# Loading and transposing the first x rows of a fused MLP backward kernel in tiles of 128, 128 and 256 rows, on two queues

## Chip, cores, metric

The kernel runs on one core of a Trainium2 chip. The metric is the device time of one execution in microseconds (us). All executions quoted here are fast: none lies over 1.5% above the fastest of its kernel. A trace starts at the first instruction of the core, and its span is about 1.8 us shorter than the execution's time.

The engines go by short names in the profiles: PE is TensorE (PEld its loading of weights), DVE is VectorE, ACT is ScalarE, POOL is GpSimd, and SP is SyncE. A load is issued by the queue of an engine, here SyncE or ScalarE; it has landed when the profile shows its last part complete. The matmuls of this kernel write to banks of the memory called PSUM, from which DVE or ACT copies the results to SBUF.

## The reference

The reference computes a two-layer MLP with SiLU and all its gradients, in bfloat16, with 2048 rows, width 640 and hidden width 1536:

```
h   = silu(x @ w1)          # x: 2048 x 640, w1: 640 x 1536
out = h @ w2                # w2: 1536 x 640
returns out, and the gradients of x, w1, w2 for a given grad_out
```

## The kernel before

The matmuls of `x @ w1` take x with its columns on the 128 partitions, so x has to be turned first. The kernel works in four chunks of 512 rows. For later chunks a transposing DMA turns x (three of them in the trace of this kernel, 7.4 us from issue to landing in the median) and TensorE does not wait for it. For the first chunk that would be too late, as an estimate from the same trace, whose first 128x512 matmul starts at 5.01 us: its rows are loaded plainly and turned on TensorE with an identity. Before they land, matmuls on a tile of ones run as a warm-up for the clock of TensorE (with them it was full from 3.6 us in the trace below). The head of the kernel is this:

```python
NWARM = 22
warm = cpool.tile([P, P], dt_in, name="warm")
early = [nc.vector.memset(warm[:], 1.0)]
for i in range(NWARM):
    early.append(nc.tensor.matmul(wp[:, 0:P], lhsT=warm[:], rhs=warm[:], start=True, stop=True))
...
def load_x_half(half):
    lo = half * 2 * P
    return nc.sync.dma_start(
        out=x_two[:, half, :, :], in_=x2[lo:lo + 2 * P, :].rearrange("(p q) d -> p q d", q=2)
    )
...
early += [load_x_half(0), load_x_half(1), load_w1_rows(0, 1), load_w1_rows(1, KM)]
load_w1_rows(KM, DT)                         # KM = 2, DT = 5 row blocks of w1
start_before_entry_wait(nc, {i.ins.name for i in early})
for fc in range(1, NFC):
    load_w1(fc * FC, (fc + 1) * FC)          # 640 KB each
...
def pe_x_half(xT, half):
    lo = half * 2 * P
    for dt_ in range(DT):
        tp = ps_h.tile([P, 2, P], dt_in, name="tp", tag="hp")
        for q in range(2):
            nc.tensor.transpose(tp[:, q, :], x_two[:, half, q, dt_ * P:(dt_ + 1) * P], ident[:])
        copy = nc.scalar.copy if dt_ % 2 else nc.vector.tensor_copy
        copy(out=xT[:, dt_, lo:lo + 2 * P].rearrange("p (s q) -> p q s", q=2), in_=tp[:])
```

The first 128x512 matmuls (`hp<-xT,w_nat`) follow: row block 0 of w1 for four output tiles, then row block 1 for the four, then the rest. `start_before_entry_wait` moves the early instructions ahead of the barrier at the start of the program.

## Time and profile before

| | us |
|---|---|
| time, median of 3 (range) | 321.21 (321.15 to 321.69) |
| span of the trace | 318.9 |
| x halves land (trace) | 3.03 and 4.00 |
| w1 row blocks 0, 1, 2-4 land | 4.34, 5.20, 6.22 |
| first 128x512 matmul starts | 5.01 |
| last matmul starts | 315.79 |

The trace is of one more execution, of 320.68 us, which is not among the three.

The page of the kernel before, its line of TensorE's busy time (busy us, share of the span, instructions) and its chain of work that ended last, by engine and by line:

```profile
PE 315.2 (99%) x1498; PEld 145.4 (46%) x1498; DVE 102.2 (32%) x182; ACT 77.7 (24%) x142; POOL 0.7 (0%) x6
...
PE 98%; DMA 1%; DVE 1%; issue 0%; DVEq 0%; SPq 0%
```

TensorE (PE) is the limit. From 5.01 us on it has no gap, so a change to the head can gain only what it takes off the start of the first 128x512 matmul. Here is that head: the timeline of PE in the kernel before from 0 to 11 us (start, length, what, count, and in brackets how long PE was idle before the group and for whom):

```profile
0.50 2.53 PE L125 MATMUL wp<-warm 128*128 128x128 bf16 x22 [0.50 <-DVE warm L121]
3.08 1.70 PE L177 MATMUL tp<-ident,x_two 128*128 128x128 bf16 x20
5.01 6.20 PE L186 MATMUL hp<-xT,w_nat 128*128 128x512 bf16 x28 [0.23 <-DVE xT L179]
```

The 22 warm-up matmuls, the 20 transposes and then the stream of 128x512 matmuls stand nearly back to back. The longest idle time that the timeline gives between them is the 0.23 us before the first 128x512 matmul, which waits for the last needed copy of DVE. One more line is needed later, from the groups by line and form of the kernel before, window 5.5 to 8.9 us (after the bar: busy us, mean ns of one):

```profile
L186 PE MATMUL hp<-xT,w_nat 128*128 128x512 bf16 x18 | 4.0, 379 | 0.0
```

A 128x512 matmul has a recorded length of 379 ns and starts come 216 ns apart: this is called full clock here. For a 128x128 matmul the starts are 56 ns apart at full clock and 107 at half. In this trace they change from 107 to 56 at 3.6 us.

### The profile page before, as it was taken

What the parts mean: (1) busy time and instruction counts of PE and PEld (TensorE: products, weight loads), DVE (VectorE), ACT (ScalarE), POOL (GpSimd) and SP (SyncE); (2) the same over time, 40 slices, a digit from 0 to 9 for tenths busy, and PEclk for the clock granted to TensorE, in tenths of its full rate; (3) what the DMA queues carried; (4) which work ended last, traced back from release to release, by engine and by line L of the source; (5) the groups of instructions that cost most, each with busy time, mean ns of one, the idle gap of its engine ahead of it and who ended that gap; (6) DMA issues with size and microseconds to landing.
All of it is one profiled execution on the core that took longest, in us unless ns stands there. A gap on an engine that the chain in (4) does not pass through costs nothing.

```text
span 318.9 us, 3570 instructions
## 1 busy us (share of the span) xinstructions
PE 315.2 (99%) x1498; PEld 145.4 (46%) x1498; DVE 102.2 (32%) x182; ACT 77.7 (24%) x142; POOL 0.7 (0%) x6
## 2 busy tenths in 40 slices
PE   9999999999999999999999999999999999999996
PEld 6444444444444444444444444444444444444443
DVE  2871641477410187700157741000001100001001
ACT  4951000644201354311065410111000001001100
POOL 0000000000000000000000000000000000000000
DMA  8999999998999866382643089719999998995011
GB/s 274 319 173 221 250 243 277 334 289 264 290 288 305 199 200 166 109 286 82 166 128 119 2 279 264 200 45 285 272 207 270 262 249 288 239 293 194 34 48 34
DMA packets 147311, 67.33 MB, mean 211 GB/s; under 512 B 112608, under 2 KB 147040, under 8 KB 147296
## 3 DMA queue, kind: packets, MB, share of 16 engines
q1 hardware_dynamic: 147296, 67.12, 81.5%
q8 instruction: 11, 0.18, 0.2%
q14 instruction: 4, 0.03, 0.0%
HBM read 9.83 MB, written 28.97 MB: 122 GB/s over the span
## 4 chain that ended last, share of the span: by engine, by line
PE 98%; DMA 1%; DVE 1%; issue 0%; DVEq 0%; SPq 0%
PE hp L249 32%; PE hp L186 16%; PE hp L337 16%; PE hp L233 16%; PE hp L385 15%; PE hp L367 1%; DMA x_two<-in_x_dram 1%; DVE xT L179 0%; PE tp L177 0%; DVE g L378 0%; DVEq L378 0%; SPq L413 0%
## 5 line engine op out<-in xcount | busy, mean ns | idle before, releaser
L186 PE MATMUL hp<-xT,w_nat 128*128 128x512 bf16 x240 | 56.9, 379 | 0.2 <-DVE xT L179 0.2
L233 PE MATMUL hp<-goT,w2T 128*128 128x512 bf16 x240 | 56.9, 379 | 0.0
L249 PE MATMUL hp<-aT,w_nat 128*128 128x512 bf16 x240 | 52.5, 379 | 0.0
L249 PE MATMUL hp<-ghT,w1T 128*128 128x512 bf16 x240 | 52.5, 379 | 0.0
L337 PE MATMUL hp<-a_blk,go_nat 128*128 128x512 bf16 x240 | 52.0, 379 | 0.0
L385 PE MATMUL hp<-gh_blk,x_nat 128*128 128x512 bf16 x224 | 48.5, 379 | 0.0
L257 ACT ACTIVATE oT<-hp 128x512 bf16<-128x512 f32 x24 | 14.3, 597 | 109.8 <-PE hp L249 109.8
L195 ACT ACTIVATE aT<-hp 128x512 bf16<-128x512 f32 x48 | 29.9, 625 | 32.8 <-PE hp L186 32.8
L186 PEld LDWEIGHTS <-w_nat 128*128 128x128 bf16 x240 | 23.5, 98 | 28.4 <-issue 0.4
L233 PEld LDWEIGHTS <-w2T 128*128 128x128 bf16 x240 | 23.5, 98 | 28.3
L337 PEld LDWEIGHTS <-go_nat 128*128 128x128 bf16 x240 | 23.5, 98 | 28.3
L249 PEld LDWEIGHTS <-w1T 128*128 128x128 bf16 x240 | 23.5, 98 | 28.3
L249 PEld LDWEIGHTS <-w_nat 128*128 128x128 bf16 x240 | 23.4, 98 | 28.3
L259 DVE CAST oT<-hp 128x512 bf16<-128x512 f32 x16 | 11.1, 692 | 77.0 <-PE hp L249 77.0
L240 DVE SCALAR_TENSOR_TENSOR ghT<-ghT,hp 128x512 bf16<-128x512 bf16 x48 | 32.5, 681 | 7.3 <-PE hp L233 7.3
L385 PEld LDWEIGHTS <-x_nat 128*128 128x128 bf16 x224 | 21.9, 98 | 26.4
L202 DVE SCALAR_TENSOR_TENSOR ghT<-aT,v 128x512 bf16<-128x512 bf16 x48 | 32.7, 686 | 0.5
L201 DVE TENSOR_SCALAR v<-t 128x512 bf16<-128x512 f32 x48 | 20.2, 425 | 30.1 <-ACT t L199 30.1
L199 ACT ACTIVATE t<-hp 128x512 f32<-128x512 f32 x48 | 29.8, 625 | 0.0
L396 DVE CAST g<-hp 128x512 bf16<-128x512 f32 x7 | 4.8, 691 | 47.1 <-PE hp L385 27.6
L347 DVE CAST g2T<-hp 128x512 bf16<-128x512 f32 x7 | 4.8, 692 | 46.1 <-PE hp L337 46.1
L345 ACT ACTIVATE g2T<-hp 128x512 bf16<-128x512 f32 x8 | 4.8, 597 | 47.0 <-PE hp L337 47.0
(20 smaller groups left out, 25.2 us busy)
## 6 DMA issues: line engine op xcount, KB each, us to landing
aT_scr<-aT SPq DMA_DIRECT2D x4, 1536.0 KB, 7.1
ghT_scr<-ghT SPq DMA_DIRECT2D x4, 1536.0 KB, 8.0
out_dram<-o_sb SPq DMA_DIRECT2D x8, 640.0 KB, 3.6
oT_scr<-oT SPq DMA_DIRECT2D x4, 640.0 KB, 3.6
go_nat<-in_grad_out_dram SPq DMA_DIRECT2D x4, 640.0 KB, 6.6
x_nat<-in_x_dram SPq DMA_DIRECT2D x4, 640.0 KB, 5.4
gxT_scr<-oT SPq DMA_DIRECT2D x4, 640.0 KB, 4.7
w_nat<-in_w_dram SPq DMA_DIRECT2D x1, 1920.0 KB, 13.7
```

The costliest lines, as they stand in the source:

```text
L186: nc.tensor.matmul(hp[:], lhsT=w1_nat[:, dt_, ft * P:(ft + 1) * P], rhs=xT[:, dt_, :], start=(dt_ == 0), stop=(dt_ == DT - 1),)
L195: nc.scalar.activation(aT[:, ft, :], hp[:], ACT.Silu)
L199: nc.scalar.activation(t[:], hp[:], ACT.Tanh, scale=0.5)
L201: nc.vector.tensor_scalar(out=v[:], in0=t[:], scalar1=-0.5, scalar2=0.5, op0=ALU.mult, op1=ALU.add)
L202: nc.vector.scalar_tensor_tensor(out=ghT[:, ft, :], in0=aT[:, ft, :], scalar=1.0, in1=v[:], op0=ALU.subtract, op1=ALU.mult)
L233: nc.tensor.matmul(gp[:], lhsT=w2T[:, dt_, ft * P:(ft + 1) * P], rhs=goT[:, dt_, :], start=(dt_ == 0), stop=(dt_ == DT - 1),)
L240: nc.vector.scalar_tensor_tensor(out=ghT[:, ft, :], in0=ghT[:, ft, :], scalar=1.0, in1=gp[:], op0=ALU.add, op1=ALU.mult)
L249: nc.tensor.matmul(op_[:], lhsT=w_all[:, ft, dt_ * P:(dt_ + 1) * P], rhs=rhs_all[:, ft, :], start=(ft == 0), stop=(ft == FT - 1),)
L257: nc.scalar.activation(oT[:, dt_, :], op_[:], ACT.Copy)
L259: nc.vector.tensor_copy(out=oT[:, dt_, :], in_=op_[:])
L337: nc.tensor.matmul(gp[:], lhsT=go_nat[:, st, dt_ * P:(dt_ + 1) * P], rhs=a_blk[:, st, :], start=(st == 0), stop=(st == ST - 1),)
L385: nc.tensor.matmul(gp[:], lhsT=x_nat[:, st, dt_ * P:(dt_ + 1) * P], rhs=gh_blk[:, st, :], start=(st == 0), stop=(st == ST - 1),)
```

## The change

Its intent is to start turning x sooner: a first tile of 128 rows needs half the bytes of the first half of before, a second queue takes part of the loads, and fewer, joint copies empty the PSUM banks. The rows land directly in `x_nat`, which needs them at the end anyway, so one later 640 KB load goes away. The load of w1 rows 2-4 also joins the early ones. The diff, cut to its core:

```diff
-    NWARM = 22
+    NWARM = 17
+    NFILL = 2
...
-        early += [load_x_half(0), load_x_half(1), load_w1_rows(0, 1), load_w1_rows(1, KM)]
-        load_w1_rows(KM, DT)
+        early += [
+            load_x_tiles(nc.sync, 0, 1),
+            load_x_tiles(nc.scalar, 1, 2),
+            load_x_tiles(nc.sync, 2, STC),
+            load_w1_rows(nc.scalar, 0, KM),
+            load_w1_rows(nc.sync, KM, DT),
+        ]
...
+        def turn(out, st, dt_):
+            nc.tensor.matmul(
+                out, lhsT=x_nat[:, st, dt_ * P:(dt_ + 1) * P], rhs=ident[:], start=True, stop=True
+            )
+
+        def pe_x_tile(xT, st):
+            for copy, lo, hi in ((nc.vector.tensor_copy, 0, KM), (nc.scalar.copy, KM, DT)):
+                tp = ps_h.tile([P, hi - lo, P], FP32, name="tp", tag="hp")
+                for dt_ in range(lo, hi):
+                    turn(tp[:, dt_ - lo, :], st, dt_)
+                copy(out=xT[:, lo:hi, st * P:(st + 1) * P], in_=tp[:])
... (pe_x_pair: two tiles as pe_x_half before, with float32 banks and plain matmuls)
-        pe_x_half(xT_next, 0)
-        pe_x_half(xT_next, 1)
+        pe_x_tile(xT_next, 0)
+        pe_x_tile(xT_next, 1)
+        for i in range(NFILL):
+            nc.tensor.matmul(wp[:, 0:P], lhsT=warm[:], rhs=warm[:], start=True, stop=True)
+        pe_x_pair(xT_next, 2)
...
-                for j in range(0, ST, STC):
+                for j in range(STC, ST, STC):      # the later load of x_nat
```

The two fillers are written between tile 1 and tiles 2-3, but they depend on nothing, and the scheduler puts them ahead of tile 0. They are two more warm-up matmuls.

More of the change, by code (lines that the diff above doesn't have):

```diff
@@ L145, with load_x_tiles, load_w1_rows @@
         xT_next = xpool.tile([P, DT, SC], dt_in, name="xT")
-        x_two = cpool.tile([P, 2, 2, D], dt_in, name="x_two")
         def load_w1(lo, hi):
             nc.sync.dma_start(out=w1_nat[:, :, lo:hi], in_=w1_v[:, :, lo:hi])
-        def load_x_half(half):
-            lo = half * 2 * P
-            return nc.sync.dma_start(
-                out=x_two[:, half, :, :], in_=x2[lo:lo + 2 * P, :].rearrange("(p q) d -> p q d", q=2)
-            )
-        def load_w1_rows(lo, hi):
-            return nc.sync.dma_start(out=w1_nat[:, lo:hi, 0:FC], in_=w1_v[:, lo:hi, 0:FC])
-        early += [load_x_half(0), load_x_half(1), load_w1_rows(0, 1), load_w1_rows(1, KM)]
-        load_w1_rows(KM, DT)
+        def load_x_tiles(eng, lo, hi):
+            return eng.dma_start(out=x_nat[:, lo:hi, :], in_=x_v[:, lo:hi, :])
+        def load_w1_rows(eng, lo, hi):
+            return eng.dma_start(out=w1_nat[:, lo:hi, 0:FC], in_=w1_v[:, lo:hi, 0:FC])
+        early += [
[5 more added lines that the diff above has]
+        ]
         start_before_entry_wait(nc, {i.ins.name for i in early})
@@ L170, with pe_x_pair @@
         nc.sync.dma_start_transpose(out=w1T[:], in_=w1[:, :])
-        def pe_x_half(xT, half):
-            lo = half * 2 * P
+        def turn(out, st, dt_):
[8 more added lines that the diff above has]
+                copy(out=xT[:, lo:hi, st * P:(st + 1) * P], in_=tp[:])
+        def pe_x_pair(xT, st):
             for dt_ in range(DT):
-                tp = ps_h.tile([P, 2, P], dt_in, name="tp", tag="hp")
+                tp = ps_h.tile([P, 2, P], FP32, name="tp", tag="hp")
                 for q in range(2):
-                    nc.tensor.transpose(tp[:, q, :], x_two[:, half, q, dt_ * P:(dt_ + 1) * P], ident[:])
+                    turn(tp[:, q, :], st + q, dt_)
                 copy = nc.scalar.copy if dt_ % 2 else nc.vector.tensor_copy
-                copy(out=xT[:, dt_, lo:lo + 2 * P].rearrange("p (s q) -> p q s", q=2), in_=tp[:])
-        pe_x_half(xT_next, 0)
-        pe_x_half(xT_next, 1)
+                copy(out=xT[:, dt_, st * P:(st + 2) * P], in_=tp[:])
+        pe_x_tile(xT_next, 0)
[3 more added lines that the diff above has]
+        pe_x_pair(xT_next, 2)
         def h_mm(hp, ft, xT, lo, hi):
```

## The prediction

> **What bounds the kernel.** The page gives PE 99% of the 318.9 us span; the chain that ended last is 98% PE. The timeline shows the first 128x512 matmul (hp<-xT,w_nat) at 5.01 us; from there to the last at 315.8 us no gap between matmul starts exceeds the 216 ns that one takes. So only the first 5.0 us are open to this change, and most of that brings x in.
>
> **The head now** (timeline, with landings): the x halves (320 KB each) are issued at 0.09 and 0.54 us and land at 3.03 and 4.00; w1 row blocks 0, 1 and 2-4 land at 4.34, 5.20 and 6.22, the next w1 block (640 KB) at 9.07. The six DVE copies stand back to back from 3.51, 0.33 us apart; the first of the second half ends at 4.96 and releases the first matmul. DMA is saturated (share 0.98 to 1.09 in windows from 6 to 12 us).
>
> **What the change does.**
> - Tile 0 is half the bytes, but tile 1 travels beside it on the ACT queue: estimate, from 320 KB landed at 3.03, first landing 2.5 to 2.9 us, second 2.8 to 3.1.
> - [...] In issue order tiles 2-3 would land near 4.0; fully interleaved with those 256 KB, near 4.7 (estimate from the rate of before). I take 4.3.
> - Plain matmuls cost what transposes cost: 128x128 warm-up matmuls and early transposes both start 107 ns apart, later transposes 56. Copies: DVE 512 float32 columns took 692 ns and 256 bf16 columns 440, so about 440 for 256 float32: no change. ACT 384 columns took 491 ns.
> - Gain: two joint copies per tile empty the DVE backlog before tiles 2-3 land. The first matmul then starts about landing + 0.05 + 0.28 (two transposes) + 0.43 (copy): 4.8 to 5.5 us, middle 5.1, against 5.01.
> - Next wait: the 21st matmul needs the w1 block that landed at 9.07, and started at 9.33. All bytes ahead of it remain, x in 1280-byte pieces instead of 2560, so it lands near 9.0 to 9.2 again. That alone caps any gain at about 0.3 us.
> - One later 640 KB reload of x goes away; PE never waited for it: worth nothing.
> - Warm-up ends near 2.5 us (19 matmuls) instead of 2.8 (22): it costs, up to about 1 us, only if PE idles long enough that full clock (seen from 3.5 us) comes late.
>
> **Prediction.** Time 321.2 us, range 320.6 to 321.9. Faster by over 2%: 0.01 (it would take 6.4 us, more than the head holds); within 2%: 0.98; slower by over 2%: 0.01.
>
> **What would show it.** First landing of x before 2.9 us; tiles 2-3 between 4.0 and 4.7; DVE idle just before the first pair copy; first 128x512 matmul within 4.7 to 5.5; either no gap or a short wait for w_nat near 9 us; then starts 216 ns apart; span within 0.6 us of 318.9.
>
> **What would make it wrong.** Two queues filling the engines faster early on than one (gain 0.3 us or more); the ACT queue starving tiles 2-3; [...] ACT's table load (1.28 us), pushed behind its two DMA issues, delaying its first copy.

"Those 256 KB" are w1 rows 0-1 on the ACT queue. 4.3 + 0.05 + 0.28 + 0.43 is 5.06 us for the first 128x512 matmul (the "middle 5.1"), against 5.01 before.

## More of the kernel before

Most sets have 5 or 6 executions, one of which carries the full trace. The sets come from several chips; each later call timed the kernel before again, eleven times, on its own chip.

## The result

The changed kernel took 322.83 us, median of 6 (321.9 to 323.46), against 321.2 (320.94 to 321.69) for the kernel before. The ratio is 1.0044 with a 95% interval of 1.0024 to 1.0064. Ratios here are the mean time of one kernel's fast runs over that of the other's of the same rounds, so they are not quite the ratio of the medians quoted. In this set the change is slower by about 1.4 us, which is outside the predicted range of 320.6 to 321.9 us.

The page of the changed kernel, the lines that answer to those of before:

```profile
PE 314.8 (98%) x1466; PEld 146.1 (45%) x1495; DVE 102.4 (32%) x181; ACT 77.9 (24%) x142; POOL 0.7 (0%) x6
...
PE 97%; DMA 2%; issue 1%; SPq 0%; DVE 0%; DVEq 0%
```

About thirty matmul records are missing from this trace; the busy time can't tell the two kernels apart. The timeline of PE in the changed kernel from 0 to 11 us can:

```profile
0.50 2.00 PE L126 MATMUL wp<-warm 128*128 128x128 bf16 x17 [0.50 <-DVE warm L122]
2.29 0.42 PE L197 MATMUL wp<-warm 128*128 128x128 bf16 x2
2.50 1.27 PE L175 MATMUL tp<-ident,x_nat 128*128 128x128 bf16 x10
5.79 1.25 PE L175 MATMUL tp<-ident,x_nat 128*128 128x128 bf16 x10 [2.02 <-DMA x_nat<-in_x_dram]
6.83 4.45 PE L202 MATMUL hp<-xT,w_nat 128*128 128x512 bf16 x14
```

The first two tiles are turned early, as intended (tile 0 landed at 2.26 us, tile 1 at 2.94). Then PE waits 2.02 us for tiles 2-3, which land at 5.74 us and not near 4. The piece of the chain of work that ended last in this window, in order of time, says the same: the chain hangs for 5.20 us on that one load.

```profile
0.55 5.20 DMA x_nat<-in_x_dram
5.74 0.05 issue
5.79 1.25 PE tp L175 x10
```

The second thing to see is the length of the groups. The ten transposes after the gap take 1.25 us, as long as the ten before it; at full clock ten take about 0.73. The groups by line and form of the changed kernel, window 5.5 to 8.9 us:

```profile
L202 PE MATMUL hp<-xT,w_nat 128*128 128x512 bf16 x5 | 2.3, 625 | 0.0
```

The mean is 625 ns where it was 379: the first five 128x512 matmuls start 427 ns apart, and full clock comes only at 8.95 us. The view of the cores gives a mean granted clock of 1.000 for both kernels, so this loss is not in that figure:

```profile
core 0: 321.7 us, clock 1.000
```

It is seen in the spacing and lengths of the matmuls. The trace also keeps records of the granted clock, which no view prints. In the changed kernel the first of them begins at 8.95 us and reads 1.00 for 314.03 us, the second, after the last matmul, reads 0.50. The mean takes the time before the first as full: PEclk reads 1.00 in each stretch of 2 us from 0 to 10 us. (The traces of the kernel before and of the first run with 14 fillers have no such record.)

The two add up to the difference between the traces. The last matmul starts at 318.67 us instead of 315.79, 2.87 us later: 1.82 from the later first 128x512 matmul (6.83 against 5.01), and five starts of 427 instead of 216 ns, 1.06. After that both streams run alike. The larger part is the late start, and most of that is the load: tiles 2-3 landed 1.74 us later than the second half of x before. This traced execution was the slowest of its six (323.46 us), and that of the kernel before (320.68 us) was faster than all six timed beside the change.

### The profile page after: what moved, and what is told of

Its sections match the earlier page's. It is cut to its first block, busy times and chain, and to the rows that moved or that the text cites. A ratio compares the mean times of both kernels' runs of the same rounds, so it can differ in the third digit from the quotient of the medians.

```text
span 321.7 us, 3534 instructions
## 1 busy us (share of the span) xinstructions
PE 314.8 (98%) x1466; PEld 146.1 (45%) x1495; DVE 102.4 (32%) x181; ACT 77.9 (24%) x142; POOL 0.7 (0%) x6
## 4 chain that ended last, share of the span: by engine, by line
PE 97%; DMA 2%; issue 1%; SPq 0%; DVE 0%; DVEq 0%
PE hp L265 32%; PE hp L202 16%; PE hp L249 16%; PE hp L353 16%; PE hp L401 15%; DMA x_nat<-in_x_dram 2%; PE hp L383 1%; PE tp L175 0%; SPq L152 0%; DVE g L394 0%; DVEq L394 0%; SPq L429 0%
```

## The experiments

Four causes were held against each other:

- **A:** the loads on the second queue hold back tiles 2-3.
- **B:** 1280-byte pieces in place of 2560 slow the load of x.
- **C:** the idle gap of PE between tile 1 and tiles 2-3 makes full clock come late.
- **D:** plain matmuls into float32 banks cost more than transposes.

### One queue

```diff
-            load_x_tiles(nc.scalar, 1, 2),
+            load_x_tiles(nc.sync, 1, 2),
...
-            load_w1_rows(nc.scalar, 0, KM),
+            load_w1_rows(nc.sync, 0, KM),
```

> The changed kernel with its first five loads all issued by SyncE in the same order (tile 0, tile 1, tiles 2-3, w1 rows 0-1, w1 rows 2-4); nothing else changed. Theory A [...]: tiles 2-3 land near 4.0 us instead of 5.74, the PE gap before their transposes shrinks from 2.0 us to under 0.6, the first 128x512 matmul starts at 4.8 to 5.0 us, time within 0.4 us of the kernel before (321.2), so about 1.5 us below the changed kernel. Rival B (1280-byte pieces and three loads are slow in themselves): tiles 2-3 land after 5 us again and the time stays near 322.8.

Measured: tiles 2-3 landed at 4.35 us and not at 5.74. (With two queues they landed at 3.96 us in the next experiment, so this one trace does not show that the queue matters.) The time did not move: 322.76 us median, executions from 321.84 to 323.5, ratio to the kernel before 1.0044, the same as the change. The expectation of about 321.2 was a clear miss, and A as the main cause fell with it. The traced execution was one of the two fastest (321.84). Its timeline of PE from 0 to 12 us:

```profile
4.40 1.15 PE L175 MATMUL tp<-ident,x_nat 128*128 128x128 bf16 x10 [0.61 <-DMA x_nat<-in_x_dram]
5.40 4.48 PE L202 MATMUL hp<-xT,w_nat 128*128 128x512 bf16 x19
10.55 1.68 PE L202 MATMUL hp<-xT,w_nat 128*128 128x512 bf16 x7 [0.67 <-DMA w_nat<-in_w_dram]
```

There is still a gap before tiles 2-3, and here the second w1 block, landing at 10.50 us, held PE for 0.67 us. That is the "next wait" of the prediction. Full clock came at 5.32 us here, before the first 128x512 matmul; the slow executions of this set have no trace.

### 36 fillers in the gap

The fillers now read the transposed tile 0, so the scheduler can't move them ahead of it (they start at 3.59 us in the trace, after tile 1):

```diff
-    NFILL = 2
+    NFILL = 36
...
-            nc.tensor.matmul(wp[:, 0:P], lhsT=warm[:], rhs=warm[:], start=True, stop=True)
+            nc.tensor.matmul(wp[:, 0:P], lhsT=warm[:], rhs=xT_next[:, 0, 0:P], start=True, stop=True)
```

> The changed kernel with 36 filler matmuls that read the transposed tile 0, so that they run between tile 1 and tiles 2-3 (the two fillers of before them are gone), loads untouched. Theory C (the 2 us of idle PE delay the full clock): PE is at full clock (56 ns between starts) from about 3.5 us, the transposes of tiles 2-3 and all 128x512 matmuls run at full clock, first 128x512 matmul still near 6.3 us if tiles 2-3 land near 5.7, and about 1.0 to 1.5 us come off 322.8. Rival (the full clock came late for another reason, such as only 17 warm-up matmuls or the plain matmuls): still 107 ns starts after the gap and no gain.

Measured: 322.68 us median, no gain. Full clock came at 5.04 us (theory C wanted 3.5), but tiles 2-3 landed at 3.96 us in this execution and had to wait until the fillers were through:

```profile
3.59 2.87 PE L197 MATMUL wp<-xT,warm 128*128 128x128 bf16 x36
6.30 0.72 PE L175 MATMUL tp<-ident,x_nat 128*128 128x128 bf16 x10
7.09 1.24 PE L202 MATMUL hp<-xT,w_nat 128*128 128x512 bf16 x5
```

The ten transposes take 0.72 us here, against 1.25 before. The fillers were too many. The run also shows that the landing of tiles 2-3 varies: 3.96 us here and 5.74 in the first trace, with the same loads.

### The kernel before with w1 row blocks 0 and 1 on the second queue

```diff
         def load_w1_rows(lo, hi):
-            return nc.sync.dma_start(...)
+            eng = nc.scalar if hi <= KM else nc.sync
+            return eng.dma_start(...)
```

> The kernel before with only w1 row blocks 0 and 1 issued by ScalarE in place of SyncE; x halves (2560-byte pieces), transposes, warm-up as before. Theory A: [...] the second half lands later than 4.00 us (4.5 to 5.7), the first 128x512 matmul moves later by as much, time up by 0.5 to 2.5 us over 321.2. Rival B (piece size, tile size): nothing changes, time within 0.2 us of 321.2.

Measured: 321.32 us median, ratio 1.0007 (0.9989 to 1.0025). The second half of x landed at 4.44 us instead of 4.00 and the first 128x512 matmul started at 5.53, but the time is not clearly different. The second queue alone does not make the loss.

### The kernel before with plain matmuls into float32 banks

```diff
-                tp = ps_h.tile([P, 2, P], dt_in, name="tp", tag="hp")
+                tp = ps_h.tile([P, 2, P], FP32, name="tp", tag="hp")
...
-                    nc.tensor.transpose(tp[:, q, :], x_two[...], ident[:])
+                    nc.tensor.matmul(tp[:, q, :], lhsT=x_two[...], rhs=ident[:], start=True, stop=True)
```

> The kernel before with its transposes as plain matmuls with the identity into float32 banks, nothing else. If plain matmuls and float32 copies cost what transposes do (all theories but one): time within 0.15 us of 321.2 and copies of 256 columns near 430 ns. Rival D (the plain matmuls are part of the loss): up by 0.3 us or more, with later full clock or longer copies.

Measured: 321.14 us median, ratio 0.9995 (0.9976 to 1.0014). D falls. From the groups by line, up to 7 us, first of this run and then of the kernel before, the copies of DVE take 442 and 439 ns:

```profile
L185 DVE CAST xT<-tp 128x256 bf16<-128x256 f32 x6 | 2.4, 442 | 3.1 <-PE tp L177 3.1
```

```profile
L179 DVE COPY xT<-tp 128x256 bf16<-128x256 bf16 x6 | 2.1, 439 | 3.1 <-PE tp L177 3.1
```

### 14 fillers in the gap

As the 36 fillers, with NFILL = 14.

> The changed kernel (two queues) with 14 fillers between tile 1 and tiles 2-3, about 1.5 us at half clock, in place of 36 (36 were too many: tiles 2-3 landed at 3.96 us in that run and waited for PE until 6.3). Theory C [...]: the slow ones near 323.3 go, all executions lie between 321.3 and 322.4, mean about 0.7 us under the changed kernel's 322.7; full clock by 5.6 us in the profile. Rival (the loss is late x alone): mean within 0.2 us of 322.7, unless x lands early.

Measured: 321.43 us median (320.79 to 322.23), ratio 1.0008 (0.9993 to 1.0023). Against the first set of the change, on another chip, most of the loss is gone, although loads, transposes and copies are those of the change. The timeline of PE:

```profile
2.68 1.25 PE L175 MATMUL tp<-ident,x_nat 128*128 128x128 bf16 x10 [0.19 <-DMA x_nat<-in_x_dram]
3.73 1.29 PE L197 MATMUL wp<-xT,warm 128*128 128x128 bf16 x14
4.96 0.73 PE L175 MATMUL tp<-ident,x_nat 128*128 128x128 bf16 x10
5.76 5.56 PE L202 MATMUL hp<-xT,w_nat 128*128 128x512 bf16 x25
```

Full clock came at 4.4 us, during the fillers. Tiles 2-3 landed late, at 4.92 us, and the first 128x512 matmul starts 0.75 us later than in the kernel before; that part of the loss stays.

### One queue and 8 fillers

The one-queue kernel with NFILL = 8, fillers as above.

> All early loads on SyncE, plus 8 fillers in the gap (0.86 us at half clock, about the gap of 0.93 us seen with one queue). Theory C: executions near 323.2 go, mean near 321.6, and what is left over 321.1 is a late second w1 block (it landed at 10.5 us and held PE for 1.05 us in the first one-queue run). Rival (the small pieces of x slow the whole load stream): mean stays over 322.2.

Measured: 321.61 us median (321.06 to 322.48), ratio 1.0014 (1.0000 to 1.0028), against 322.76 without the fillers (on another chip). Again most of the loss goes. In the trace tiles 2-3 landed at 4.67 us, and PE waited for the first w1 rows, which landed at 6.09, until 6.14.

### The kernel before without warm-up

```diff
-    NWARM = 22
+    NWARM = 0
```

> The kernel before with no warm-up matmuls at all, so PE is idle until x lands near 3.0 us; loads and the rest untouched. Theory C: the clock goes to full [...] between 5.5 and 9 us, the early 128x512 matmuls run 427 ns apart until then, and the time rises by 0.8 to 1.7 us over 321.1, which is the size of the loss of the change. Rival (clock plays no part): within 0.2 us of 321.1.

Measured: 321.53 us median (321.2 to 322.61), ratio 1.0012 (0.9998 to 1.0027); means 321.66 against 321.26. This was expected to cost 0.8 to 1.7 us and cost about 0.4, not clear of noise. In the trace full clock came between 6.1 and 6.4 us, so only two 128x512 starts and part of a third were at half clock. Without any warm-up, PE begins at 3.16 us and from then on is busy almost without a pause. In this trace an unbroken stretch of work just before the stream did nearly what the warm-up does.

### The kernel before with 1280-byte pieces

```diff
-  in_=x2[lo:lo + 2 * P, :].rearrange("(p q) d -> p q d", q=2)
+  in_=x2[lo:lo + 2 * P, :].rearrange("(q p) d -> p q d", p=P)
...
-  copy(out=xT[:, dt_, lo:lo + 2 * P].rearrange("p (s q) -> p q s", q=2), in_=tp[:])
+  copy(out=xT[:, dt_, lo:lo + 2 * P].rearrange("p (q s) -> p q s", q=2), in_=tp[:])
```

> The kernel before with each 256-row half of x loaded as two 128-row tiles side by side (1280-byte pieces, as in the change) in place of two neighbouring rows per partition (2560-byte pieces); same two loads, same queue, same transposes, copies without the stride. Theory B (small pieces slow the load of x): x halves land 0.2 to 0.5 us later than 3.0 and 4.0, time up by 0.3 to 0.8. If pieces do not matter: within 0.15 us of 321.1.

Measured: 321.12 us median, ratio 1.0000 (0.9988 to 1.0012). The halves landed at 3.08 and 3.97 us. B falls. A side result is that the DVE copies, no longer strided at the output, took 292 ns instead of 439; the time shows nothing of it.

### The change again, 14 fillers again, 30 warm-up matmuls, and tile 1 alone on the second queue

> The changed kernel once more, unedited, on the same chip as the next three, for a second trace and a same-chip comparison. Theory C: mean again 1.2 to 1.6 us over the kernel before; PE idle for over 0.8 us between tile 1 and tiles 2-3; executions spread over 1 us or more.

Measured: 321.19 us median, 320.79 to 322.92, ratio 1.001 (0.999 to 1.0029). The expected 1.2 to 1.6 us did not come: five of the six executions took 320.79 to 321.47 us. Only the traced one was slow (322.92), and its timeline of PE is this:

```profile
2.51 1.27 PE L175 MATMUL tp<-ident,x_nat 128*128 128x128 bf16 x10
4.67 1.25 PE L175 MATMUL tp<-ident,x_nat 128*128 128x128 bf16 x10 [0.89 <-DMA x_nat<-in_x_dram]
6.26 5.11 PE L202 MATMUL hp<-xT,w_nat 128*128 128x512 bf16 x17 [0.34 <-DMA w_nat<-in_w_dram]
```

So the loss is not the same in each execution; the change has good and bad ones. Full clock came at 8.42 us here.

> The kernel with 14 fillers once more. Theory C: 0.8 to 1.4 us under the changed kernel of the same call, 0.1 to 0.4 over the kernel before. If the first result was luck: no difference from the changed kernel.

Measured: 321.64 us median (320.99 to 321.79), ratio 1.0014 (1.0001 to 1.0027). Against the change on the same chip this is no gain in the mean (321.54 against 321.40), because the change itself was late only once there. The expectation missed. None of the five with fillers was slow and one of the six without was, which by itself shows nothing.

For the third kernel NWARM went from 17 to 30 and NFILL from 2 to 0:

> The changed kernel with 30 warm-up matmuls in front and no fillers: tile 0 waits in SBUF until about 3.7 us, its transposes and those of tile 1 then run to about 4.8, so the idle gap before tiles 2-3 closes from the other side. Loads, transposes and copies are those of the change. Theory C (only the idle gap matters, not where it is filled): time within 0.3 us of the kernel with 14 fillers, so about 1 us under the changed kernel, although the first two tiles are transposed over 1 us later. Rival (what counts is early transposes, or the place of the fillers): no gain over the changed kernel.

Measured: 321.35 us median, 321.26 to 321.54, a narrow set; ratio 1.0008 (0.9995 to 1.0021). Its timeline of PE:

```profile
0.50 3.38 PE L126 MATMUL wp<-warm 128*128 128x128 bf16 x30 [0.50 <-DVE warm L122]
3.67 2.14 PE L175 MATMUL tp<-ident,x_nat 128*128 128x128 bf16 x20
5.77 2.53 PE L202 MATMUL hp<-xT,w_nat 128*128 128x512 bf16 x10
```

Tile 0 was turned over 1 us later than in the change, yet the time agrees with that of the 14 fillers. Turning the first tiles early is worth nothing that can be seen, nor does it seem to matter where the gap is closed. The expected 1 us under the change did not come in this call: the means are 321.36 against 321.40 us, since the change had only its one slow execution here.

For the fourth kernel, w1 rows 0-1 went back to SyncE behind tiles 2-3, tile 1 stayed on the ScalarE queue, and NFILL was 6, fillers as above:

> Tile 1 alone on the ScalarE queue; w1 rows 0-1 follow tiles 2-3 on SyncE; 6 fillers in the gap. Theory A in its weak form (w1 rows 0-1 on the second queue delay tiles 2-3, which costs what is left of the loss once the gap is filled): tiles 2-3 land by 4.2 us, first 128x512 matmul at 4.8 to 5.1, time 0 to 0.3 us under the kernel before. If the landing of tiles 2-3 is scattered whatever stands on the second queue: no better than the 14 fillers.

Measured: 321.42 us median (320.83 to 324.13), ratio 1.002 (0.9993 to 1.0047). Tiles 2-3 landed at 3.78 us, the earliest of all traces. But w1 rows 0-1 landed at 5.27 us, and the first 128x512 matmul started only at 5.31. In this trace, what one load gains the next one loses. It is not faster than the kernel before; one execution of 324.13 us has no trace (its granted clock is taken up below).

### The change twice more, and a late x on purpose

> The changed kernel, unedited, third set. Theory C: executions spread from about 320.8 to 323.5 us; if the traced one is under 321.7, its matmuls start 56 or 216 ns apart (full clock) from 5.6 us at the latest; if it is over 322.5, full clock comes after 7.5 us.

Measured: 321.4 us median, executions of 320.74, 321.02, 321.08, 321.71, 323.74 and 324.63. The traced one was fast (321.08):

```profile
2.70 1.15 PE L175 MATMUL tp<-ident,x_nat 128*128 128x128 bf16 x10
4.58 0.73 PE L175 MATMUL tp<-ident,x_nat 128*128 128x128 bf16 x10 [0.72 <-DMA x_nat<-in_x_dram]
5.47 5.77 PE L202 MATMUL hp<-xT,w_nat 128*128 128x512 bf16 x25 [0.16 <-ACT xT L192]
```

This pair shows what the clock costs. Compare it with the slow traced execution of the same kernel above (322.92 us, on another chip). In both, tiles 2-3 land at nearly the same time (4.53 and 4.63 us). The fast one turns them in 0.73 us, the slow one in 1.25. The first 128x512 matmul starts at 5.47 against 6.26. Of these 0.79 us, 0.09 are the landing, 0.42 the slower transposes (first start to last), and the rest, 0.27, goes with a wait for w1 rows 0-1 in the slow one, which landed at 6.22 us. Then five starts at half clock add 1.06. Together that is 1.85 us, and the times differ by 1.84. So the clock cost about 1.5 us in this pair, and the loads the rest.

> As the third set: the same kernel for one more trace and six more times; a traced execution under 321.7 has full clock by 5.6 us, one over 322.5 has it after 7.5 us.

Measured: 322.68 us median (321.63 to 323.33), ratio 1.0045 (1.0028 to 1.0061). In the traced execution (321.63 us) tiles 2-3 landed at 3.98 us, and full clock came at 6.42 us, later than the 5.6 expected of a fast one: three starts at half clock, a case between the two.

For the last pair, tiles 2-3 were put behind w1 rows 2-4 on the SyncE queue, once with the change's own NFILL = 2 and once with 22 fillers that read the transposed tile 0:

```diff
-            load_x_tiles(nc.sync, 2, STC),
             load_w1_rows(nc.scalar, 0, KM),
             load_w1_rows(nc.sync, KM, DT),
+            load_x_tiles(nc.sync, 2, STC),
```

> The changed kernel with tiles 2-3 on purpose behind w1 rows 2-4 on the SyncE queue, so that they land near 6 us in every execution and PE is idle for over 2 us. Theory C: full clock comes between 7.5 and 10 us in most executions; first 128x512 matmul near 7 us; time 323.0 to 324.4. Rival (late x alone costs, the clock does not): about 322.8, no more than the 1.8 us by which the first matmul is later.

Measured: 324.5 us median; executions of 323.7 to 324.91, and the traced one of 322.54, the fastest of the set. In it full clock had been reached at 4.37 us, before the transposes of tiles 2-3, which is not what was expected of most executions, and the long gap did not take it away again:

```profile
6.04 0.73 PE L175 MATMUL tp<-ident,x_nat 128*128 128x128 bf16 x10 [2.10 <-DMA x_nat<-in_x_dram]
6.94 3.40 PE L202 MATMUL hp<-xT,w_nat 128*128 128x512 bf16 x14 [0.16 <-ACT xT L192]
```

The other five, 1.2 to 2.4 us slower with the same loads, have no trace. That they had full clock late is likely for some; two of them (324.35 and 324.66 us) had it and seem to have lost it again, as estimated below.

> The same late load of tiles 2-3 with 22 fillers in the gap (2.35 us at half clock). Theory C: full clock by 5.7 us, first 128x512 matmul still near 6.8, time 0.6 to 1.6 us under the same kernel without fillers. Rival (late x alone costs): the two agree within 0.3 us.

Measured: 323.3 us median (322.5 to 325.06). The means are 323.43 against 324.16, so the fillers take 0.7 us off, at the lower end of what was expected, with scatter of the same size. In the trace full clock was reached at 3.96 us, as expected. But tiles 2-3 landed at 6.80 us and not near 6, and the first 128x512 matmul started at 7.65. A late x costs too, of itself; here more than the clock.

### The change and 14 fillers once more on one chip

> The changed kernel, fifth set, beside its version with fillers. Theory C: between one and five of six executions over 322.4 us (11 of 24 so far), mean 321.4 to 322.7.

Measured: 322.33 us median; executions of 321.1, 321.47, 321.48, 323.18, 323.76 and 325.05. In the traced one (323.18) full clock came at 9.22 us, after a gap of over 1 us and eight starts at half clock:

```profile
4.99 1.25 PE L175 MATMUL tp<-ident,x_nat 128*128 128x128 bf16 x10 [1.09 <-DMA x_nat<-in_x_dram]
6.03 4.12 PE L202 MATMUL hp<-xT,w_nat 128*128 128x512 bf16 x11
```

> The version with 14 fillers, third set, same chip. Theory C: no execution over 322.4 us (0 of 11 so far), mean 321.3 to 321.6, and full clock by 5.6 us in the trace. If fillers do not matter: about as many executions over 322.4 as the changed kernel has in this call.

Measured: 321.92 us median (321.25 to 322.36), ratio to the kernel before 1.0014 (0.9994 to 1.0035), means 321.84 against 322.67 of the change. Full clock came at 3.95 us:

```profile
3.71 1.07 PE L197 MATMUL wp<-xT,warm 128*128 128x128 bf16 x14
4.61 0.72 PE L175 MATMUL tp<-ident,x_nat 128*128 128x128 bf16 x10
5.58 6.65 PE L202 MATMUL hp<-xT,w_nat 128*128 128x512 bf16 x29 [0.25 <-DMA w_nat<-in_w_dram]
```

The mean was expected up to 321.6; no execution was over 322.4, as expected, though three came within 0.3 us of it.

### All sets together

The limit of 322.4 us was chosen after the first sets, because it parts the groups:

| kernel | executions | over 322.4 us | mean us |
|---|---|---|---|
| before (all sets it was timed in, with the first) | 61 | 1 | 321.24 |
| the change, five sets | 30 | 14 | 322.29 |
| the change with 14 fillers, three sets | 17 | 0 | 321.63 |
| the change with 30 warm-up matmuls | 5 | 0 | 321.36 |

On average the change costs 1.05 us (322.29 less 321.24). The fillers give back 0.66 of it; 0.39 stays. The sets come from different chips, so the split is rough. The medians of the five sets of the change are 322.83, 321.19, 321.4, 322.68 and 322.33 us. The one execution of the kernel before over 322.4 (322.72) has a span of only 319.8 us, so most of its excess lies outside the span.

And the five traces of the changed kernel. Full clock is from the clock records; the last two columns split the delay of the last matmul against the trace of the kernel before:

| trace | time us | tiles 2-3 land | full clock from | first 128x512 | its delay | lost after it |
|---|---|---|---|---|---|---|
| third set | 321.08 | 4.53 | 3.62 | 5.47 | 0.46 | 0.00 |
| fourth set | 321.63 | 3.98 | 6.42 | 5.07 | 0.06 | 0.68 |
| second set | 322.92 | 4.63 | 8.42 | 6.26 | 1.25 | 1.06 |
| fifth set | 323.18 | 4.94 | 9.22 | 6.03 | 1.02 | 1.59 |
| first set | 323.46 | 5.74 | 8.95 | 6.83 | 1.82 | 1.05 |

What is lost after the first 128x512 matmul is all half clock. On the mean of these five it is 0.88 us, beside 0.92 us of later start, and in the last four rows a part of the start is the clock's too, since there tiles 2-3 are turned in 1.25 us instead of 0.73.

Why is the clock late in some executions only? The traces show when it came, not why. Starts change from 107 to 56 or from 427 to 216 ns at once, at a different time in each trace. 18 of the 20 traces have clock records, and in these, full clock lasted either 314.03 us (12 traces) or 317.44 us (6) until it fell back after the last matmul; what sets these lengths is not shown.

In four traces with fillers in the gap full clock came at 3.95, 3.96, 4.4 and 5.04 us (14, 22, 14 and 36 fillers), in the kernel before at 3.6. In the five traces of the change PE has, between the starts on either side of the gap, about 0.95, 0.49, 1.20, 1.39 and 2.33 us (third, fourth, second, fifth and first set), and full clock came at 3.62, 6.42, 8.42, 9.22 and 8.95 us. So in the first of them it was there before the gap, and in the other four it came only after tiles 2-3 were turned, latest in the three with the longest gaps. The gap alone doesn't decide it: with tiles 2-3 late on purpose full clock came at 4.37 us, inside a gap of 2.4 us. Which executions are hit, and how much work of PE brings full clock, is not shown.

A late clock is not all. Six executions, none with a trace, have a mean granted clock of 0.995: 323.5 us (one queue), 323.76 (the change), 324.13 (tile 1 alone on the second queue), 324.35 and 324.66 (late x) and 325.06 (late x with fillers). None of the 55 executions of the kernel before whose clock is on record reads under 0.999. In the traces the mean never reads under 0.999, since it counts only the fall after the last matmul. As an estimate from these figures, 0.005 of about 324 us is 1.6 us lost, or some 3.2 us at half clock (the starts take twice as long there, 427 against 216 ns), for which full clock, once reached, seems to have been taken away again. Where and why has no trace, so that stays open.

## Why the prediction was wrong

- **What bounds the kernel** was right: after the head the streams run alike, and the whole difference of 2.87 us between the first two traces arose before 9 us.
- **The step that failed was the last term, the clock.** The prediction named it: "Warm-up ends near 2.5 us (19 matmuls) instead of 2.8 (22): it costs, up to about 1 us, only if PE idles long enough that full clock (seen from 3.5 us) comes late." It was then left out of the sum, and a later full clock stood only under what would make it wrong. In four of the five traces of the change the first 128x512 matmuls ran at half clock, and 14 of 30 executions were over 322.4 us. The cause is not that the warm-up is shorter: no execution with 30 matmuls or with 14 fillers was over 322.4 us (0 of 22), and the kernel before with no warm-up at all lost only about 0.4 us. The sets point to the gap that the change opens between tile 1 and tiles 2-3, 0.5 to 2.3 us between starts in the traces; how it delays the clock is not shown. The prediction had the parts to see it: tile 1 turned by about 3.6 us, tiles 2-3 "I take 4.3". And the size was too small: in the traced pair about 1.5 us (1.06 in 128x512 starts, 0.42 in slower transposes), and in the fifth set 1.59 us in 128x512 starts alone.
- **"I take 4.3"** for the landing of tiles 2-3 was too early for the first trace (5.74), where it made the larger part of the delay (1.82 of 2.87 us is the later start), and near the median of all five (4.63). What was missed is the scatter, 3.98 to 5.74. That it comes from the second queue is not shown: with one queue tiles 2-3 landed at 4.35 and 4.67 us, with tile 1 alone on the second queue at 3.78. The 0.4 us that stay with the fillers have no single cause in their traces: the first 128x512 matmul (5.76, 5.96 and 5.58 us) came late after tiles 2-3 in the first (landed at 4.92), after the fillers themselves in the second (tiles landed at 4.51 and were turned from 5.04), and after w1 rows 0-1 in the third (landed at 5.54).
- **"First landing 2.5 to 2.9"** was 2.26; earlier than predicted and worth nothing, as the 30 warm-up matmuls showed.
- **"Plain matmuls cost what transposes cost ... no change"** was right (ratio 0.9995).
- **DVE idle before the first pair copy** was right (2.3 us in the waits of the changed kernel) and no gain: the backlog of DVE was replaced by a wait for the DMA.
- **The first 128x512 matmul "within 4.7 to 5.5"** was at 6.83; of the five traces of the change, two are within that range.
- **The "next wait"** near 9 us did not show in the change's first trace, since its start was too late to meet it. It showed in the one-queue run (0.67 us).
- The change's range was also taken too narrow for a kernel whose executions are spread over 4 us, 320.74 to 325.05. With another set the number could have come out right by luck: two of the five medians, 321.19 and 321.4, lie within the range. The missing term would have been missing all the same.

No version tried is clearly faster than the kernel before. The best executions of the change (320.74) and of the kernel before (320.56) are about equal, so the early transposes bought nothing. Where x came sooner in a trace, PE met the next load instead: w1 rows 0-1 with tile 1 alone on the second queue, the next w1 block with one queue.

## What to carry to other kernels

Before a long stream of matmuls, keep TensorE working until full clock has come (here no execution with 14 fillers or 30 warm-up matmuls was over 322.4 us, 0 of 22, against 14 of 30 of the change); splitting a load so that the first piece is used early can open a pause between the pieces (here 0.5 to 2.3 us between starts). Fillers must depend on something that keeps them in the gap, or the scheduler moves them to the front (here to 2.29 us, ahead of tile 0), and they must be about as long as the gap and not longer (36 of them held tiles 2-3, landed at 3.96 us, until 6.30). Where a head of a few microseconds is at stake, take several traces and look at all executions: one trace shows one of at least two courses, and a mean granted clock of 1.000 doesn't tell them apart.

## What else these traces show

- Pauses of PE before full clock went with a late clock: in three traces of the change, gaps of 1.2 to 2.3 us between starts went with full clock only at 8.42 to 9.22 us. In the one trace of the late x (322.54 us) full clock came at 4.37 us, inside a gap of 2.4 us, and was still there after it; but two executions of the same set (324.35 and 324.66 us), with a mean granted clock of 0.995, seem to have lost it again for some 3 us (the estimate above).
- The profile's mean granted clock can read 1.000 while the first 128x512 matmuls start 427 instead of 216 ns apart. The clock records begin only with the first change (8.95 us in the first trace of the change).
- Plain matmuls with the identity in place of transposes made no difference in time in this head: 321.14 against 321.11 us, and both start 107 ns apart at half clock.
- With the change's loads tiles 2-3 landed at 3.96 to 5.74 us in ten traces. The second half of x on a single queue landed at 3.92 to 4.00 in four; but the three loads of x on a single queue brought tiles 2-3 at 4.35 and 4.67, so the second queue is not shown to be the cause.
